# The first stage of an attention and mixture-of-experts kernel: a written order for VectorE, scores one unit ahead, weight conversions spread evenly

## The chip, the cores and the metric

The kernel runs on one core of a Trainium2 chip. The metric is the device time of one execution in microseconds (us); smaller is better. A unit of attention work below is half a batch (four heads); there are 16.

## The reference

```python
def sm_attn(qq, kk, vv):
    s = scale * np.matmul(qq, kk.transpose(0, 1, 3, 2))
    s = s - np.max(s, axis=-1, keepdims=True)
    a = np.exp(s)
    a = a / (np.sum(a, axis=-1, keepdims=True) + 1e-09)
    return np.matmul(a, vv)
p_packed = sm_attn(p, k, v)                 # 8 batches, 8 heads, 32 x 576 scores
out = sm_attn(q, p_packed, p_packed)
...
h = x @ w_in                                # 4608 x 512 x 2048
x = (h - np.tanh(h)) @ w_out
...
# top-2 of 8 experts, from x @ w_gate plus noise scaled with x @ w_noise:
h = np.maximum(x[mask] @ w1[e], 0.0)
out[mask] += top2_w[mask, k, None] * (h @ w2[e])
```

`w_in` and `w_out` come as 8-byte floats. The chip's engines work on 4-byte floats, so the kernel makes those from the two 4-byte words of each number by bit operations.

## The kernel before

There are three stages. The first (`phase_a`) computes `p_packed` for all 16 units and, beside it, converts 28 of the 32 chunks of `w_in` and `w_out` (128 x 512 numbers each, the "widenings"). The second (`phase_b`) does the other attention, the dense layer and the routing in steps; the third (`PhaseC`) is the experts. From some steps into the second stage on, TensorE (PE) works almost without a pause.

A unit of the first stage goes through these steps: `load_k` and `load_v` (SyncE, SP, issues the DMAs), `s1` (PE: 16 score matmuls into PSUM), `max1` (VectorE, DVE: a maximum over 576 columns and a scaling by -0.125), `exp1` (ScalarE, ACT), `recip1` (DVE, two instructions on 128 x 1), `t1` (PE: six transposes), `a1t` (ACT: copy of these to SBUF), `pv` (PE), `pz2` (DVE: scales `pv` into `Pz`), `pt` (PE transpose), `pt_out` (ACT copy into `PT`) and `pt_store` (a DMA). A chunk is `cv_load` (a DMA of 512 KB into `cvr`), part 0 (ACT, absolute value, line 69), part 1 (DVE, lines 73, 75, 76, 78 and 80), part 2 (ACT, line 84) and part 3 (DVE, lines 88 and 91).

`phase_a` runs a loop over `n`. In each turn of it the steps in the string `ORDER` are called in that order: the back half of unit n-1 (`t1` to `pts`), the front half of unit n, and the parts of two chunks, `p0` to `p3` for the first and `r0` to `r3` for the second; `pl` and `rl` load the two chunks of the next turn. `manual_schedule(engines=ENG)` keeps the written order on the engines in `ENG`. On every other engine a scheduler places the instructions, and before the change DVE is one of these. The 28 chunks go into the turns 0 to 13, two in each; the turns 14 and 15 have none.

Some buffers matter. The PSUM pool `psb` has two buffers under one tag for the scores `s1` and the transposes `tp`. `kT` and `v` have two buffers each, the raw chunks `cvr` have three.

`qs`, `qm`, `qx` and `qa` are the steps of the second attention's first block, in the turns 3 and 5 to 8: two PE score groups `sq`, DVE transposes into `st`, a maximum `mq` (DVE), a subtraction on GpSimd (POOL), an exponential (ACT), a sum (DVE), a multiplication (POOL) and a last transpose (DVE).

`consts_b` makes small constants for the routing. In the second stage's todo list its first part stands at step 1 and the rest, DMAs that fill two DRAM tensors, at step 3. In that stage `u_mm` (PE) fills both buffers of the PSUM pool `pm`, `u_hi` (ACT) and `u_lo` (DVE, tile `ul`) empty them, and `wo_step` widens the last four chunks (`cvc_b`, `cvf_b`).

Of the kernel before, what the change touches and what calls it, by code (L numbers as in the profile page):

```python
# [10 lines left out]
F32 = mybir.dt.float32  # L11
# [10 lines left out]
P = 128  # L22
# [78 lines left out]
    e.tensor_tensor(lo, src, hi.bitcast(F32), op=ALU.subtract)  # L101


ORDER = """t1 a1t s1 p0 lk p1 max1 p2 p4 pl r4 rec pv pz2 p3 exp1 pt r0 pto pts qs r1 lv qm qx r2 r3 qa rl""".split()
ENG = {mybir.EngineType.PE, mybir.EngineType.SP, mybir.EngineType.Activation}
NWA = 12


def phase_a(K, kT, v, w_in, w_out, wide_in, wide_out):
# [4 lines left out]
    with ExitStack() as ctx:  # L114
# [117 lines left out]
        def on(n, *fs):  # L232
            if 0 <= n < 16:
                for f in fs:
                    f(n)
# [5 lines left out]
              6: (lambda: Q.max(0), lambda: Q.sub(0), lambda: Q.exp(0)),  # L241
              7: (lambda: Q.sum(0), lambda: Q.mul(0)),
              8: (lambda: Q.out(0),)}
        load_k(0)
        cv_load(0)
        load_k(1)
        cv_load(1)
        load_v(0)
        for n in range(18):
            c0, c1 = 2 * n, 2 * n + 1  # L250
            ops = {
                "s1": lambda: on(n, s1), "max1": lambda: on(n, max1), "exp1": lambda: on(n, exp1),
                "t1": lambda: on(n - 1, t1), "a1t": lambda: on(n - 1, a1t), "rec": lambda: on(n - 1, recip1),
                "pv": lambda: on(n - 1, pv), "pz2": lambda: on(n - 1, pz2), "pt": lambda: on(n - 1, pt),
                "pto": lambda: on(n - 1, pt_out),
                "qs": lambda: n in (3, 5) and [f() for f in qs[n]], "qm": lambda: n == 6 and [f() for f in qs[n]],
                "qx": lambda: n == 7 and [f() for f in qs[n]], "qa": lambda: n == 8 and [f() for f in qs[n]],
                "pts": lambda: on(n - 1, pt_store),
                "lk": lambda: on(n + 2, load_k), "lv": lambda: on(n + 1, load_v),
                "p4": lambda: None, "r4": lambda: None,  # L260
                "p0": lambda: cv_step(c0, 0), "p1": lambda: cv_step(c0, 1), "p2": lambda: cv_step(c0, 2), "p3": lambda: cv_step(c0, 3),
                "r0": lambda: cv_step(c1, 0), "r1": lambda: cv_step(c1, 1), "r2": lambda: cv_step(c1, 2), "r3": lambda: cv_step(c1, 3),
                "pl": lambda: cv_load(c0 + 2) if c0 + 2 < 16 + NWA else None, "rl": lambda: cv_load(c1 + 2) if c1 + 2 < 16 + NWA else None,
            }
            for o in ORDER:
                ops[o]()
# [82 lines left out]
NSURE = 75  # L349


def consts_b(K, pp, pq, zero, w_gate, w_noise):
    nc, cp = K.nc, K.cpool
    K.tri = cp.tile([96, 96], BF, name="tri")
    nc.vector.memset(K.tri, 1.0)
# [17 lines left out]
    K.quarter = cp.tile([P, 1], F32, name="quarter")  # L373
    for q in range(4):
        nc.vector.memset(K.quarter[32 * q:32 * q + 32], float(q))
    pre = pq.tile([P, P, 2], F32, tag="st", name="pre")
    nc.vector.memset(pre, 0.0)
    nc.gpsimd.iota(pre[:, :, 0], pattern=[[1, P]], base=N, channel_multiplier=0, allow_small_or_imprecise_dtypes=True)
    yield
    tv = K.table.rearrange("(r l) two -> r (l two)", l=P)  # L380
    for r in range(0, TROWS, P):
        n = min(P, TROWS - r)
# [4 lines left out]
def pool(K, stack, name, bufs, **kw):  # L387
    return stack.enter_context(K.tc.tile_pool(name=name, bufs=bufs, reuse_waits="tile", **kw))


def phase_b(K, stack, wo_stack, qT, w1, w2, w_out, wide_out, noise, w_gate, w_noise, out):
# [7 lines left out]
    stage = stack.enter_context(ExitStack())  # L399
    K.WI = pool(K, stage, "b_wi", 1, side="right").tile([P, 4, FF], F32, name="WI")  # L400
    Q = K.Q = Queries(K, qT, qp, wq, None)
    yield
    RAW, CVB = {}, {}

# [12 lines left out]
    with ExitStack() as ctx:  # L417
# [4 lines left out]
        gp = pool(K, ctx, "b_g", 4)  # L422
        Q.pools = pool(K, ctx, "b_a", 2)
        wp = pool(K, ctx, "b_w", 1)
        cpre = pool(K, ctx, "b_pre", 1)
        wo2 = pool(K, ctx, "b_wo", 16 - NWA)

        woh = wp.tile([P, 16, DM], FR, name="woh")
        wol = []

        zero = wp.tile([P, P], F32, name="zero")
        nc.vector.memset(zero, 0.0)
        ET = mybir.EngineType
        ctx.enter_context(tc.manual_schedule(engines={ET.PE, ET.Activation, ET.DVE, ET.SP}))
        UT, GT, ACC, LG, PACE = {}, {}, {}, {}, [None]
# [243 lines left out]
        def at(t, f, *args):  # L679
            todo.setdefault(t, []).append((f, args))  # L680
# [36 lines left out]
            wol.append((wo2 if i < 16 - NWA else K.wo_pool).tile([P, DM], FR, tag="wo", name=f"wol{i}"))  # L717
            split(K, woh[:, i], wol[i], K.wof[i], "act", "pool" if i % 2 else "dve")

        consts = consts_b(K, cpre, wq, zero, w_gate, w_noise)  # L720
        at(1, next, consts)
        at(3, next, consts, None)

        def wo_step(i, p):
# [545 lines left out]
```

## Time and profile before

| | before |
|---|---|
| median of 3 runs | 1775.44 us (1774.39 to 1779.5) |
| the profiled execution, its own time | 1771.26 us |
| its span from the first to the last instruction | 1769.5 us |
| mean granted TensorE clock over the span | 0.956 of full |
| first stage, from the start to the last `Pz` | 0 to 146.34 us |
| first DVE instruction of the second stage on `ul` | 148.45 us |

The profiled execution is 4.18 us below the median of the runs. Times in the trace count from the start of the span. In a row of the timeline the first number is the start and the second the duration, both in us; a bracket at the end tells how long the engine sat idle before it and what ended that.

### The profile page before, as it was taken

How to read it: one execution, taken by the hardware profiler on the slowest of the kernel's cores; microseconds unless marked ns; L12 is line 12 of the kernel's file. 1: busy time of each engine (PE TensorE's matmuls, PEld its weight loads, DVE VectorE, ACT ScalarE, POOL GpSimd, SP SyncE). 2: the span in 40 equal slices, each digit the busy share in tenths (PEclk: the TensorE clock that was granted, in tenths of full speed). 3: DMA queues.
4: the chain of work that ended last, by engine and by line, in shares of the span. 5: the costliest groups of instructions: out<-in, count | busy, mean ns of one | idle time of the engine just before them, and what ended most of it. 6: DMA issues, size and time to landing. Idle time of an engine off the chain costs nothing. (4 is left out here: it accounts for less than half of the span.)

```text
span 1769.5 us, 29373 instructions
## 1 busy us (share of the span) xinstructions
PE 1633.7 (92%) x9942; PEld 1384.1 (78%) x9942; DVE 1198.9 (68%) x3090; ACT 871.1 (49%) x1850; POOL 569.2 (32%) x557
## 2 busy tenths in 40 slices
PE   5667999999999999999569699999999999999996
PEld 3345899898989898989557588888888888888885
DVE  7896978887878788866257366666666666666652
ACT  3454555555555555543134255555555555555552
POOL 0001200121212121223524644555454444444421
PEclk8668999999999999999779899999999999999998
DMA  8783467787867687722132656523672236722631
GB/s 275 237 271 109 131 218 228 218 241 213 242 223 229 213 239 219 238 95 83 23 112 43 233 176 196 152 48 56 230 238 49 49 67 220 239 50 49 206 62 26
DMA packets 145079, 285.22 MB, mean 161 GB/s; under 512 B 19618, under 2 KB 69066, under 8 KB 140316
## 3 DMA queue, kind: packets, MB, share of 16 engines
q1 hardware_dynamic: 121100, 243.78, 41.8%
q0 software_dynamic: 23824, 39.51, 12.3%
q8 instruction: 80, 1.31, 0.3%
q14 instruction: 75, 0.61, 0.1%
HBM read 687.34 MB, written 107.59 MB: 449 GB/s over the span
## 5 line engine op out<-in xcount | busy, mean ns | idle before, releaser
L1068 PE MATMUL ph<-w0s,xh 128*128 128x512 f32 x1200 | 378.5, 397 | 10.2 <-DVE h L1070 9.6
L1086 ACT ACTIVATE ht<-h 32x256 f32<-32x256 f32 x600 | 249.2, 415 | 267.4 <-issue 131.2
L1101 PE MATMUL py<-w1s,hh 128*128 128x512 f32 x1200 | 371.2, 390 | 2.3 <-ACT hh L97 2.3
L930 POOL DMA_INDIRECT x<-x1d,gidxm x276 | 265.4, 961 | 315.4 <-DVE xt L939 249.0
L500 PE MATMUL acc<-gh,woh 128*128 128x288 f32 x1024 | 302.9, 296 | 7.7 <-issue 7.6
L500 PE MATMUL acc<-gh,wol 128*128 128x288 f32 x1024 | 303.1, 296 | 7.0 <-issue 6.8
L500 PE MATMUL acc<-gl,woh 128*128 128x288 f32 x1024 | 301.9, 295 | 4.7 <-issue 4.7
L1070 DVE STREAM_TRANSPOSE h<-ph 128x512 f32<-128x512 f32 x150 | 107.4, 716 | 281.8 <-PE ph L1068 235.5
L1068 PEld LDWEIGHTS ph<-w0s,xh 128*128 128x128 f32 x1200 | 227.3, 190 | 64.3 <-DVE h L1070 11.2
L1101 PEld LDWEIGHTS py<-w1s,hh 128*128 128x128 f32 x1200 | 225.9, 188 | 50.9 <-ACT hh L97 3.2
L1068 PE MATMUL ph<-w0s,xl 128*128 128x512 f32 x600 | 236.8, 395 | 1.7 <-issue 1.7
L1101 PE MATMUL py<-w1s,hl 128*128 128x512 f32 x600 | 235.4, 392 | 2.1 <-DVE hl L101 1.3
L665 POOL DMA_INDIRECT table<-d,qi x96 | 91.8, 956 | 384.1 <-DVE g L484 151.6
L500 PEld LDWEIGHTS acc<-gl,woh 128*128 128x128 f32 x1024 | 193.5, 189 | 7.6 <-issue 7.6
L500 PEld LDWEIGHTS acc<-gh,woh 128*128 128x128 f32 x1024 | 193.7, 189 | 7.3 <-issue 7.3
L500 PEld LDWEIGHTS acc<-gh,wol 128*128 128x128 f32 x1024 | 193.3, 189 | 7.3 <-issue 7.3
L1084 DVE TENSOR_SCALAR ht<-h 32x256 f32<-32x256 f32 x600 | 185.7, 310 | 11.1
L97 ACT ACTIVATE gh<-g 128x288 fp32r<-128x288 f32 x256 | 113.5, 443 | 145.9 <-DVE g L484 143.9
L482 ACT ACTIVATE t<-h 128x288 f32<-128x288 f32 x256 | 104.1, 407 | 132.6 <-PE h L475 98.7
L475 PE MATMUL h<-a2h,uh 128*128 128x288 f32 x512 | 159.3, 311 | 9.8 <-DVE g L484 7.0
L484 DVE TENSOR_TENSOR g<-h,t 128x288 f32<-128x288 f32 x256 | 115.3, 450 | 61.2 <-ACT t L482 49.7
L475 PE MATMUL h<-a2l,uh 128*128 128x288 f32 x512 | 152.0, 297 | 1.1 <-issue 1.1
(235 smaller groups left out, 2495.6 us busy)
## 6 DMA issues: line engine op xcount, KB each, us to landing
w0s<-wsp SPq DMA_DIRECT2D x140, 2048.0 KB
w1s<-wsp SPq DMA_DIRECT2D x140, 2048.0 KB
wsp<-wt SPq DMA_DIRECT2D x128, 512.0 KB
wt<-in_w_dram SPq DMA_DIRECT2D x128, 256.0 KB
kT<-in_kT_dram SPq DMA_DIRECT2D x16, 608.0 KB
out_dram<-zero SPq DMA_DIRECT2D x37, 256.0 KB
v<-in_v_dram SPq DMA_DIRECT2D x16, 576.0 KB
q<-in_qT_dram SPq DMA_DIRECT2D x32, 288.0 KB
```

The costliest lines, as they stand in the source:

```text
L97: nc.scalar.activation(hi, src, AF.Copy)
L475: nc.tensor.matmul(h[:, :TN], u[:, G, fs], x[:, G, :], start=(n == 0), stop=(n == 5))
L482: nc.scalar.activation(t, h[:, :TN], AF.Tanh)
L484: PACE[0] = nc.vector.tensor_tensor(g, h[:, :TN], t, op=ALU.subtract).ins
L500: nc.tensor.matmul(ACC[ch][d][:, :TN], w[:, d * P:(d + 1) * P], x, start=(f == 0 and n == 0), stop=(f == 15 and n == 2))
L665: ins = nc.gpsimd.indirect_dma_start(out=K.table, out_offset=IO(ap=qi[:, i:i + 1], axis=0), in_=d[:, i, :], in_offset=None, oob_is_err=True)
L930: g = K.nc.gpsimd.indirect_dma_start(out=x[:, b, :], out_offset=None, in_=rows, in_offset=IO(ap=gidx[:, c, b:b + 1], axis=0))
L1068: K.nc.tensor.matmul(p, xx[:, d * P:(d + 1) * P], w[:, fc, ws, d, :], start=(n == 0), stop=(n == 11))
L1070: V.transpose(h[:, 2 * fc:2 * fc + 2].rearrange("p g n -> p (g n)"), p)
L1084: V.tensor_scalar(dst, src, 0.0, None, op0=ALU.max)
L1086: K.nc.scalar.activation(dst, src, AF.Relu)
L1101: K.nc.tensor.matmul(p, xx[:, f * P:(f + 1) * P], w[:, f // 4, ws, f % 4, :], start=(n == 0), stop=(n == 23))
```

## The change

It does four things in the first stage. DVE joins the engines that keep the written order, with a new `ORDER`. Turn n now issues `s1` of unit n+1, after `a1t` of unit n-1; `s1(0)` comes before the loop. `chunks(n)` gives each of 16 turns one or two chunks: one in the turns 0, 4, 8 and 12, two in the others. And the routing constants are made before the first stage, with only the `pre` tile (a memset and an iota) left at step 3.

```diff
-ORDER = """t1 a1t s1 p0 lk p1 max1 p2 p4 pl r4 rec pv pz2 p3 exp1 pt r0 pto pts qs r1 lv qm qx r2 r3 qa rl""".split()
-ENG = {mybir.EngineType.PE, mybir.EngineType.SP, mybir.EngineType.Activation}
+ORDER = """p0 lk pl t1 p1 a1t qm max1 s1 p2 pv r0 p3 exp1 rl lv r1 qx rec pz2 pt r2 pto pts qs r3 qa""".split()
+ENG = {mybir.EngineType.PE, mybir.EngineType.SP, mybir.EngineType.Activation, mybir.EngineType.DVE}
...
+        def chunks(n):
+            lo, hi = (min(16 + NWA, (16 + NWA) * k // 16) for k in (n, n + 1))
+            return tuple(lo + i if lo + i < hi else None for i in range(2))
+
         load_k(0)
         cv_load(0)
         load_k(1)
-        cv_load(1)
+        cv_load(chunks(0)[1])
         load_v(0)
-        for n in range(18):
-            c0, c1 = 2 * n, 2 * n + 1
+        s1(0)
+        for n in range(17):
+            c0, c1 = chunks(n)
+            d0, d1 = chunks(n + 1)
             ops = {
-                "s1": lambda: on(n, s1), "max1": lambda: on(n, max1), "exp1": lambda: on(n, exp1),
+                "s1": lambda: on(n + 1, s1), "max1": lambda: on(n, max1), "exp1": lambda: on(n, exp1),
...
-                "pl": lambda: cv_load(c0 + 2) if c0 + 2 < 16 + NWA else None, "rl": lambda: cv_load(c1 + 2) if c1 + 2 < 16 + NWA else None,
+                "pl": lambda: cv_load(d0), "rl": lambda: cv_load(d1),
...
     for q in range(4):
         nc.vector.memset(K.quarter[32 * q:32 * q + 32], float(q))
-    pre = pq.tile([P, P, 2], F32, tag="st", name="pre")
+    yield
+    pre = pp.tile([P, P, 2], F32, tag="st", name="pre")
     nc.vector.memset(pre, 0.0)
     nc.gpsimd.iota(pre[:, :, 0], pattern=[[1, P]], base=N, channel_multiplier=0, allow_small_or_imprecise_dtypes=True)
-    yield
...
     Q = K.Q = Queries(K, qT, qp, wq, None)
+    zero = wq.tile([P, P], F32, name="zero")
+    nc.vector.memset(zero, 0.0)
+    consts = consts_b(K, wq, zero, w_gate, w_noise)
+    next(consts)
     yield
...
-        consts = consts_b(K, cpre, wq, zero, w_gate, w_noise)
-        at(1, next, consts)
         at(3, next, consts, None)
```

DVE in a turn of the first stage before the change, from the `Pz` of unit 3 on; the chunk's parts stand among each other and among the unit's own steps:

```order
L216 SCALAR_TENSOR_TENSOR Pz_393<-pv_380,rs_318,mask 128x128
L75 TENSOR_SCALAR cva_365<-cvc_360 128x512
L192 TENSOR_SCALAR rs_398<-rs_398 128x1
L76 SCALAR_TENSOR_TENSOR cva_365<-cvr_296,cva_365 128x512
L193 RECIPROCAL rs_398<-rs_398 128x1
L80 TENSOR_SCALAR cvt_370<-cva_365 128x512
L88 TENSOR_TENSOR cvf_368<-cvf_368,cvt_370 128x512
L180 TENSOR_REDUCE nm_457<-s_4_436 128x1
L91 TENSOR_TENSOR WI<-cvf_368,cva_365 128x512
L73 TENSOR_SCALAR cvc_402<-cvc_402 128x512
L78 TENSOR_SCALAR cvf_416<-cvr_340 128x512
L75 TENSOR_SCALAR cva_413<-cvc_402 128x512
```

DVE after the change, the second half of turn 2 and the beginning of turn 3:

```order
L73 TENSOR_SCALAR cvc_331<-cvc_331 128x512
L75 TENSOR_SCALAR cva_343<-cvc_331 128x512
L76 SCALAR_TENSOR_TENSOR cva_343<-cvr_258,cva_343 128x512
L78 TENSOR_SCALAR cvf_346<-cvr_258 128x512
L80 TENSOR_SCALAR cvt_348<-cva_343 128x512
L194 TENSOR_SCALAR rs_256<-rs_256 128x1
L195 RECIPROCAL rs_256<-rs_256 128x1
L218 SCALAR_TENSOR_TENSOR Pz_352<-pv_318,rs_256,mask 128x128
L88 TENSOR_TENSOR cvf_346<-cvf_346,cvt_348 128x512
L91 TENSOR_TENSOR WI<-cvf_346,cva_343 128x512
L73 TENSOR_SCALAR cvc_362<-cvc_362 128x512
L75 TENSOR_SCALAR cva_376<-cvc_362 128x512
```

Now an instruction mostly reads what the one ahead of it wrote, and the next turn's first widening stands right behind this turn's last.

PE at the beginning of the first stage before the change:

```order
L175 MATMUL s_0_133<-kT_123 32x288 x8
L199 MATMUL tp_182<-ident,a_0_162 96x128 x6
L175 MATMUL s_1_191<-kT_127 32x288 x8
L211 MATMUL pv_220<-v_131,a1T_189 64x128 x12
L221 MATMUL pt_240<-ident,Pz_233 128x128
L199 MATMUL tp_262<-ident,a_1_237 96x128 x6
L175 MATMUL s_2_271<-kT_144 32x288 x8
```

And after it:

```order
L177 MATMUL s_0_157<-kT_149 32x288 x8
L177 MATMUL s_1_183<-kT_153 32x288 x8
L201 MATMUL tp_208<-ident,a_0_195 96x128 x6
L177 MATMUL s_2_228<-kT_168 32x288 x8
L213 MATMUL pv_238<-v_155,a1T_223 64x128 x12
L223 MATMUL pt_274<-ident,Pz_272 128x128
L201 MATMUL tp_288<-ident,a_1_255 96x128 x6
```

The scores of unit 2 now follow the transposes of unit 0, not those of unit 1. Since `s_1` is still held then, `s_2` takes the buffer of `tp` of unit 0 and waits until `a1t` on ACT has copied it.

DVE some steps into the second stage before the change, from the second `g` up to `ul` of the second `u`:

```order
L484 TENSOR_TENSOR g_1_1497<-h_1_1488,t_1_1495 128x288
L355 MEMSET tri 96x96
L358 MEMSET ones 96x128
L362 TENSOR_SCALAR ebase<-eio 128x8
L364 TENSOR_SCALAR eio_1508<-eio 128x8
...
L375 MEMSET quarter 32x1 x4
L377 MEMSET pre 128x256
L73 TENSOR_SCALAR cvc_b_1463<-cvc_b_1463 128x512
...
L450 TENSOR_TENSOR ul_1_1481<-u_1_0_1470,uh_1_1480 128x512
```

And after it:

```order
L492 TENSOR_TENSOR g_1_1518<-h_1_1509,t_1_1516 128x288
L73 TENSOR_SCALAR cvc_b_1484<-cvc_b_1484 128x512
L75 TENSOR_SCALAR cvc_b_1484<-cvc_b_1484 128x512
L76 SCALAR_TENSOR_TENSOR cvc_b_1484<-wor_1482,cvc_b_1484 128x512
L78 TENSOR_SCALAR cvf_b_1523<-wor_1482 128x512
L80 TENSOR_SCALAR cvf_b_1523<-cvc_b_1484 128x512
L458 TENSOR_TENSOR ul_1_1502<-u_1_0_1491,uh_1_1501 128x512
```

Twelve instructions on constants have left this place; the memset of `pre` now stands behind the fourth `g`.

## Rows read from the trace of the kernel before

**Rows 1.** Busy time of the engines in two stretches, TensorE clock, DMA share, GB/s

```profile
5.84:139.36 133.52, 84.58 (x686) 52.20 (x679) 115.89 (x278) 59.77 (x116) 2.68 (x2) 0.71 0.81 261
139.36:148.45 9.09, 7.72 (x92) 4.33 (x90) 2.10 (x9) 3.62 (x9) 0.00 (x0) 1.00 0.68 177
```

**Rows 2.** What DVE waited for from 5 to 148 us: in total, times, longest

```profile
DVE nm L180 <- PE s L175: 15.0, 11, 1.7
```

**Rows 3.** Timeline of DVE, first stage, instructions in a row

```profile
9.92 0.42 DVE L73 TENSOR_SCALAR cvc<-cvc 128x512 f32<-128x512 f32 x1
10.25 0.69 DVE L88 TENSOR_TENSOR cvf<-cvf,cvt 128x512 f32<-128x512 f32 x1
10.85 0.42 DVE L75 TENSOR_SCALAR cva<-cvc 128x512 int32<-128x512 int32 x1
...
15.51 0.42 DVE L73 TENSOR_SCALAR cvc<-cvc 128x512 f32<-128x512 f32 x1
15.97 0.43 DVE L75 TENSOR_SCALAR cva<-cvc 128x512 int32<-128x512 int32 x1
...
17.62 0.69 DVE L88 TENSOR_TENSOR cvf<-cvf,cvt 128x512 f32<-128x512 f32 x1
18.34 0.69 DVE L91 TENSOR_TENSOR WI<-cvf,cva 128x512 f32<-128x512 f32 x1
```

**Rows 4.** Timeline of DVE, the end of the first stage

```profile
140.93 0.76 DVE L180 TENSOR_REDUCE nm<-s 128x1 f32<-128x576 f32 x1 [1.40 <-PE s L175]
141.72 0.15 DVE L181 TENSOR_SCALAR nm<-nm 128x1 f32<-128x1 f32 x1
142.37 0.35 DVE L216 SCALAR_TENSOR_TENSOR Pz<-pv,rs,mask 128x128 f32<-128x128 f32 x1 [0.50 <-PE pv L211]
...
146.34 0.35 DVE L216 SCALAR_TENSOR_TENSOR Pz<-pv,rs,mask 128x128 f32<-128x128 f32 x1 [3.14 <-PE pv L211]
```

**Rows 5.** Timeline of all engines around the `Pz` of unit 1

```profile
26.09 0.35 DVE L216 SCALAR_TENSOR_TENSOR Pz<-pv,rs,mask 128x128 f32<-128x128 f32 x1 [0.60 <-PE pv L211]
26.36 0.42 DVE L75 TENSOR_SCALAR cva<-cvc 128x512 int32<-128x512 int32 x1
...
26.50 0.47 PE L221 MATMUL pt<-ident,Pz 128*128 128x128 f32 x1 [0.45 <-DVE Pz L216]
...
26.76 1.49 PE L199 MATMUL tp<-ident,a 128*96 128x128 f32 x6
...
27.01 0.28 ACT L226 ACTIVATE PT<-pt 128x128 f32<-128x128 f32 x1 [0.52 <-PE pt L221]
```

**Rows 6.** Timeline of ACT and SP: third chunk's first part, a constant's DMA issue

```profile
14.45 0.68 ACT L69 ACTIVATE cvc<-cvr 128x512 f32<-128x512 f32 x1 [3.31 <-DMA cvr<-in_w_in_dram]
...
144.83 0.50 SPq L369 DMA_DIRECT2D wgraw<-in_w_noise_dram  x1
```

**Rows 7.** Timeline of PE and ACT: scores, transposes' copy and `pv` of one unit

```profile
60.94 2.15 PE L175 MATMUL s<-kT 64*32 64x288 f32 x16
...
61.98 0.79 ACT L204 ACTIVATE a1T<-tp 96x768 f32<-96x768 f32 x1
...
63.02 2.19 PE L211 MATMUL pv<-v,a1T 96*64 96x128 f32 x24
```

**Rows 8.** Timeline of PE, POOL and DVE: the second attention's first block

```profile
58.35 1.21 PE L299 MATMUL sq<-q,pt 64*32 64x288 f32 x16
...
65.05 1.53 POOL L315 TENSOR_TENSOR st<-st,mq 128x576 f32<-128x576 f32 x1 [60.64 <-DVE mq L311]
...
65.48 1.38 DVE L78 TENSOR_SCALAR cvf<-cvr 128x512 int32<-128x512 int32 x1
```

**Rows 9.** Timeline of DVE and PE at the second stage's beginning

```profile
154.07 1.19 DVE L362 TENSOR_SCALAR ebase<-eio 128x8 f32<-128x8 f32 x1
...
158.34 1.28 DVE L450 TENSOR_TENSOR ul<-u,uh 128x512 fp32r<-128x512 f32 x2
...
159.08 1.06 PE L441 MATMUL u<-WI,pt 64*32 64x512 f32 x1 [6.10 <-DVE ul L450]
```

More of the change, by code (lines that the diff above doesn't have):

```diff
@@ L134, in cv_load @@
         def cv_load(i):
+            if i is None:
+                return
             if i < 16:
@@ L259, in phase_a @@
                 "lk": lambda: on(n + 2, load_k), "lv": lambda: on(n + 1, load_v),
-                "p4": lambda: None, "r4": lambda: None,
                 "p0": lambda: cv_step(c0, 0), "p1": lambda: cv_step(c0, 1), "p2": lambda: cv_step(c0, 2), "p3": lambda: cv_step(c0, 3),
                 "r0": lambda: cv_step(c1, 0), "r1": lambda: cv_step(c1, 1), "r2": lambda: cv_step(c1, 2), "r3": lambda: cv_step(c1, 3),
-                "pl": lambda: cv_load(c0 + 2) if c0 + 2 < 16 + NWA else None, "rl": lambda: cv_load(c1 + 2) if c1 + 2 < 16 + NWA else None,
+                "pl": lambda: cv_load(d0), "rl": lambda: cv_load(d1),
             }
@@ L349, with consts_b @@
 NSURE = 75
-def consts_b(K, pp, pq, zero, w_gate, w_noise):
+def consts_b(K, pp, zero, w_gate, w_noise):
     nc, cp = K.nc, K.cpool
@@ L424, in phase_b @@
         wp = pool(K, ctx, "b_w", 1)
-        cpre = pool(K, ctx, "b_pre", 1)
         wo2 = pool(K, ctx, "b_wo", 16 - NWA)
@@ L429, in phase_b @@
         wol = []
-        zero = wp.tile([P, P], F32, name="zero")
-        nc.vector.memset(zero, 0.0)
         ET = mybir.EngineType
```

## The prediction

> **What bounds the kernel now.** The list of the chain that ended last begins in the experts and says nothing of the first stage, so I read that stage by windows, then DVE's waits, then single instructions. In the first stage DVE is the fullest engine, 115.9 of 133.5 us, with the DMA engines 0.81 busy at 261 GB/s and PE at a mean granted clock of 0.71, a mix of 1.2 and 2.4 GHz [rows 1]. Most of what DVE loses there is 15.0 us in 11 waits of `max1` for the scores [rows 2]. After the last widening, from 139.36 us on, DVE has almost nothing left, and two units drain one behind the other. Then the second stage starts, with a hole on PE. After that PE has hardly a pause, so what the time up to there loses or gains should reach the end one to one. The question is when the last `Pz` comes, now 146.34 us, and how long the hole is.
>
> **What an instruction costs DVE.** Starts show that a step that doesn't read its predecessor's output costs less than one that does. Unrelated, a 512-wide integer or scalar step takes 0.33 us start to start (9.92 to 10.25) and a two-input step 0.60 (10.25 to 10.85). Reading the step ahead, line 75 starts 0.46 after line 73, and line 91 starts 0.72 after line 88 [rows 3]. The scheduler's order mixes chunks, and pays mostly the lower prices; the written order puts a chunk's steps in a row. Front of a chunk (73, 75, 76, 78, 80): 0.46 + 0.46 + 0.61 + 0.33 + 0.34 = 2.20, where the 0.61 is line 76 ahead of an unrelated step (0.60 by the row). Back (88, 91): 0.72 + 0.60 = 1.32. `max1`: 0.79, the scaling waiting for the whole reduction (140.93 to 141.72), and 0.12, its length of 0.15 less some overlap with an unrelated step [rows 4]. `recip1`: two such steps of 0.15, each with the 0.04 after its end that a dependent step waits (15.97 less 15.51 and 0.42), 0.38. `Pz`: 0.27 to the next start [rows 5]. A chunk is 3.52 and a unit 1.56, against 3.13 and about 1.19 at the unrelated prices. Over 28 chunks and 16 units the written order adds 10.9 + 5.9 = 16.8 us of DVE time. That takes back what the removed 15.0 us of score waits give.
>
> **A turn after the change.** I count from a `Pz` (time Z) to the next. DVE goes on with the back of the second chunk until Z + 0.27 + 1.32 = 1.59. The next front needs ACT's line 69, which in the written order stands behind `pt_out`, which needs `pt`, which needs this `Pz`: `pt` starts at Z + 0.41 and `PT` at Z + 0.92 with PE at 1.2 GHz [rows 5], about 0.1 earlier at 2.4 GHz; 0.18 later line 69 starts, takes 0.68 [rows 6], and DVE starts about Z + 1.76. Two-chunk turn: 1.76 + 2.20 + 0.91 + 1.32 + 2.20 + 0.38 = 8.77. One-chunk turn: 1.76 + 2.20 + 0.91 + 1.32 + 0.38 = 6.57 on DVE. But there PE may be later: `t1` runs from Z + 0.67 to 2.16 [rows 5], the copy `a1t` (0.79) must end before `s1` may have its buffer, then come `s1` (2.15) and `pv` (2.19) [rows 7], with overlaps about Z + 7.4 at 1.2 GHz. At 2.4 GHz DVE is later. I take 7.0 as the mean.
>
> **The start.** The first chunk comes as before, some 0.9 us later for the two constants' DMA issues (0.50 the second, the first a little shorter) ahead of it. The second chunk is no longer loaded in front; it stands behind the third `kT`, where the third chunk stood, whose line 69 started at 14.45 [rows 6]. One chunk of 524,288 bytes less is ahead of it: 261/0.81 = 322 GB/s at full share, so 1.6 us earlier, and 0.9 later. Line 69 starts about 13.75, DVE 14.45, and the first `Pz` comes 7.01 later, at 21.5. DVE idles some 2 us ahead of it.
>
> **The second attention's block** stands on DVE in the written order too. Turn 5: the transposes wait for `sq` (1.21) behind `pt`, +2.3. Turn 6: `mq`, then POOL's 1.53, ACT's exponential (some 0.7, as line 69 over nearly as many columns) and line 84 behind it before DVE's back of the first chunk, +2.8. Turn 7: reduction, two small steps, and POOL's second operation, which stretches a DVE step as line 78 here from about 0.45 to 1.38 [rows 8], +1.5. Turn 9: one split, +0.7. Sum 7.3; if ACT and POOL hide better, 2.5.
>
> **The sum.** The 15th `Pz` comes in turn 15: 21.5 + 11 x 8.77 + 3 x 7.0 + 7.3 = 146.3. One unit drains after it: 4.0 us at 2.4 GHz as in the rows (142.37 to 146.34) [rows 4], 5.4 at 1.2, taken as 4.7. So the last `Pz` is at 151.0, 4.7 later than now. The first `u` matmuls stand behind `pt` now, +0.2. In the hole, 6.1 us now, the constants leave the path to `ul`: `ebase` starts at 154.07, takes 1.19 because POOL works on a tile then, and `ul` comes at 158.34 and frees PE at 159.08 [rows 9]. The widening that moves up meets the same POOL work (as line 78 did), so I take 1.2 us saved and not the full 2.7 that the constants span. Small edits cost nothing: the constants' memsets at the start run before any chunk is there, cover 5 us; `pre`'s memset moves behind a `g`, and its DMAs are read only by scatters far later. Net: 4.7 + 0.2 - 1.2 = +3.7 us. From the profiled execution's 1771.26 that is 1775.0; this execution is 4.18 below the median of the runs, so 1779.1, rounded 1779. A measurement can tell about 0.3%, 5.3 us, from no change: I forecast no change, on the slow side. With the bounds of start, POOL, clock and drain, this case alone holds 1774 to 1785. Chance 0.62.
>
> **A rule against the prices.** The rows show 0.46 against 0.33 and 0.72 against 0.60 [rows 3]. The Trainium skill, page "VectorE: DVE Perf Modes", section "The DRAIN you can't avoid", says that the next step starts only when the pipe is empty, and that eight copies took the same with a semaphore after each as with one at the end, so that order would be free. By that rule the 0.39 per chunk and 0.37 per unit vanish, and the time would be that of rival one.
>
> **Rivals.** *One: neighbours cost nothing.* A turn is then 1.76 + 1.93 + 0.73 + 1.20 + 1.93 + 0.12 = 7.67, eleven of them save 12.1, the short ones 1.2 (PE holds them), the start 1.0: 3.7 - 14.3 = -10.6, 1765, faster. The rows speak against it. Chance 0.08. *Two: the waits hide.* The second block costs 2.5 and not 7.3, short turns 6.6, the drain 4.0 at 2.4 GHz: 3.7 - 4.8 - 1.2 - 0.7 = -3.0, 1772. For it speaks that PE was at full clock from 139 us on [rows 1]. Chance 0.16, a quarter of it faster. *Three: the loads bind.* SP issues in order, and the next `kT` and chunk stand behind `pt_store`, which waits for ACT at the turn's end. A two-chunk turn moves 622,592 + 2 x 524,288 + 589,824 + 65,536 = 2.33 MB, 7.2 us at 322 GB/s, under 8.77; it binds below 265 GB/s, and the stage's mean is 261 with gaps [rows 1]. At 240 a turn takes 9.7, and 14 turns add 13: 1792, slower. Chance 0.14, nearly all of it slower.
>
> **How the numbers follow.** Of the main case 0.18 lies beyond +5.3 us and 0.44 within. Slower: 0.18 + 0.12 = 0.30. Faster: 0.08 + 0.04 = 0.12. Same: 0.58. The range 1768 to 1788 leaves out half of rivals one and three and a little of the main case's ends.
>
> **What would show it.** `Pz` to `Pz` about 8.8 us in two-chunk turns and about 7 in the others; DVE waiting for ACT's line 69 some 0.2 us in most turns and 1.5 after a short one; no waits for scores; the first `Pz` near 21.5 and the last near 151; line 75 0.46 behind line 73. In the second stage the hole should be near 5 us. Wrong would make it: chunks that land late (DVE waits behind ACT's wait for DMA), or turns nearer 7.7.

## The result and the profile after

The changed kernel takes 1786.26 us (median of 18 runs, 1778.47 to 1791.69), the kernel before 1774.7 us on the same chips (18 runs, 1765.22 to 1779.5). The ratio is 1.0072, 95% interval 1.0058 to 1.0085: slower by 0.7%, about 12.8 us (the two medians lie 11.6 apart). The profiled execution has a span of 1784.8 us.

Chips differ by over 2% (the kernel before has a median of 1733 us on one and 1770 us on another), so kernels timed on different chips are compared by their ratio to the kernel before on the same chip. Times of the first stage agree better between chips: turns that an edit does not touch come out nearly the same (8.82 and 8.68 us for the second and third turn here and in e4 below, 8.81 and 8.67 in e12). I follow three marks through it: the `Pz` of units 0 to 15, the last of them, and the first `u` matmul behind the hole on PE, called u_2 below (159.08 us in [rows 9]). The stretch between the last two `Pz` is called the drain, the one from the last `Pz` to u_2 the handover.

The windows of the changed kernel (start:end, length, busy time and instructions of PE, PEld, DVE, ACT and POOL, granted clock, DMA share, GB/s), beside [rows 1]:

```profile
8.29:154.22 145.93, 92.31 (x726) 58.52 (x727) 123.22 (x282) 62.83 (x119) 2.31 (x2) 0.70 0.78 246
154.22:163.38 9.16, 7.44 (x44) 3.07 (x42) 0.58 (x4) 1.71 (x4) 0.00 (x0) 0.50 0.05 14
```

The first stage has become 12 us longer while the DMA engines moved less per us, and the stretch behind the last widening runs at a granted clock of 0.50, that is 1.2 GHz, where before it ran at 1.00.

What DVE waited for from 5 to 165 us (in total, times, longest), beside [rows 2]:

```profile
DVE cvc L73 <- ACT cvc L69: 14.4, 9, 5.2
DVE Pz L218 <- PE pv L213: 6.7, 4, 4.1
DVE ul L458 <- ACT uh L454: 4.5, 1, 4.5
DVE st L313 <- PE sq L306: 1.8, 1, 1.8
DVE cvf L88 <- ACT cvf L84: 1.7, 1, 1.7
```

The 15.0 us of waits for scores are gone. In their place stand waits for ACT's line 69. The first, 3.64 us, is the load of the first chunk; the longest, 5.2 us, is new.

The timeline of DVE in the first turn, beside [rows 3]:

```profile
8.29 0.43 DVE L73 TENSOR_SCALAR cvc<-cvc 128x512 f32<-128x512 f32 x1 [3.64 <-ACT cvc L69]
8.75 0.43 DVE L75 TENSOR_SCALAR cva<-cvc 128x512 int32<-128x512 int32 x1
9.21 0.69 DVE L76 SCALAR_TENSOR_TENSOR cva<-cvr,cva 128x512 int32<-128x512 int32 x1
9.82 0.42 DVE L78 TENSOR_SCALAR cvf<-cvr 128x512 int32<-128x512 int32 x1
10.16 0.42 DVE L80 TENSOR_SCALAR cvt<-cva 128x512 int32<-128x512 int32 x1
...
11.35 0.68 DVE L88 TENSOR_TENSOR cvf<-cvf,cvt 128x512 f32<-128x512 f32 x1
12.07 0.69 DVE L91 TENSOR_TENSOR WI<-cvf,cva 128x512 f32<-128x512 f32 x1
```

The written order pays 0.46, 0.46 and 0.72 us where a step reads its predecessor's output, as counted. Five two-chunk turns without other work take 8.68 to 8.84 us from `Pz` to `Pz`; the turns 13 and 14, also without, take 9.20 and 9.23.

The timeline of SP and ACT around chunk 8:

```profile
40.93 0.33 SPq L232 DMA_DIRECT2D ptd<-PT  x1
41.35 0.38 SPq L287 DMA_DIRECT2D pt<-ptd  x1
41.78 1.31 SPq L294 DMA_DIRECT2D q<-in_qT_dram  x2
43.13 0.60 SPq L162 DMA_DIRECT2D kT<-in_kT_dram  x1
43.83 0.84 SPq L146 DMA_DIRECT2D cvr<-in_w_in_dram  x2
...
51.93 0.66 ACT L69 ACTIVATE cvc<-cvr 128x512 f32<-128x512 f32 x1 [3.78 <-DMA cvr<-in_w_in_dram]
```

Line 69 of chunk 8 waits 3.78 us for its chunk. That was issued at 43.83, behind three loads for the second attention (`pt`, and `q` in two pieces) that `ORDER` puts at the end of the turn before.

The timeline of DVE and PE at the end of the stage, beside [rows 4] and [rows 9]:

```profile
152.54 0.35 DVE L218 SCALAR_TENSOR_TENSOR Pz<-pv,rs,mask 128x128 f32<-128x128 f32 x1
...
158.54 0.35 DVE L218 SCALAR_TENSOR_TENSOR Pz<-pv,rs,mask 128x128 f32<-128x128 f32 x1 [4.06 <-PE pv L213]
...
163.38 1.29 DVE L458 TENSOR_TENSOR ul<-u,uh 128x512 fp32r<-128x512 f32 x2 [4.50 <-ACT uh L454]
...
165.39 1.96 PE L449 MATMUL u<-WI,pt 64*32 64x512 f32 x16
...
173.81 2.55 PE L449 MATMUL u<-WI,pt 64*32 64x512 f32 x16 [3.89 <-DVE ul L458]
```

The last `Pz` comes at 158.54, 12.20 later than before, and u_2 at 173.81, 14.73 later. The wait ahead of u_2 fell from 6.10 to 3.89 us, but the way from the last `Pz` to it grew from 12.74 to 15.27. The rest of the program keeps the loss: 14.73 at u_2, 15.2 between the two profiled executions at the end, and 12.8 by the ratio.

### The profile page after: what moved, and what is told of

Read it like the earlier page. It is cut to its first block, busy times and chain, and to the rows that moved or that the text cites. A ratio compares the mean times of both kernels' runs of the same rounds, so it can differ in the third digit from the quotient of the medians.

```text
span 1784.8 us, 29376 instructions
## 1 busy us (share of the span) xinstructions
PE 1645.2 (92%) x9942; PEld 1389.9 (78%) x9942; DVE 1205.6 (68%) x3090; ACT 872.9 (49%) x1850; POOL 567.5 (32%) x557
## 4 chain that ended last, share of the span: by engine, by line
PE 77%; DVE 13%; issue 3%; DMA 2%; ACT 2%; another core or an unknown queue 1%; POOL 1%; SPq 0%; DVEq 0%; POOLq 0%; ACTq 0%
PE ph L1074 21%; PE py L1107 21%; PE acc L508 19%; PE h L483 10%; PE u L449 2%; DVE cva L76 1%; DVE xl L101 1%; DMA cvr<-in_w_in_dram 1%; PE sq L306 1%; DVE g L492 1%; DVE ht L1090 1%; DVE cva L75 1%; DVE cvf L88 1%; DVE gl L101 1%
## 5 line engine op out<-in xcount | busy, mean ns | idle before, releaser
L1074 PEld LDWEIGHTS ph<-w0s,xh 128*128 128x128 f32 x1200 | 226.7, 189 | 64.6 <-DVE h L1076 10.5
L1090 DVE TENSOR_SCALAR ht<-h 32x256 f32<-32x256 f32 x600 | 185.9, 310 | 11.1
```

What stands on the lines that cost most here:

```text
L1074: K.nc.tensor.matmul(p, xx[:, d * P:(d + 1) * P], w[:, fc, ws, d, :], start=(n == 0), stop=(n == 11))
L1090: V.tensor_scalar(dst, src, 0.0, None, op0=ALU.max)
```

## The experiments

Each was timed beside the kernel before: e2 to e5 together on one chip, e1 and e6 to e8 together, e9 to e11 together, e12 by itself. u_2 is read from the profiled execution.

| kernel | ratio to before, 95% | last Pz, us | u_2, us |
|---|---|---|---|
| changed kernel | 1.0072 (1.0058 to 1.0085) | 158.54 | 173.81 |
| e1 constants alone | 0.9999 (0.9988 to 1.0010) | 146.96 | 158.31 |
| e2 no spread | 1.0058 (1.0041 to 1.0075) | 154.06 | 166.28 |
| e3 scheduler's DVE order | 1.0005 (0.9993 to 1.0017) | 148.05 | 163.07 |
| e4 late q | 1.0056 (1.0039 to 1.0072) | 154.46 | 169.74 |
| e5 interleaved | 1.0119 (1.0099 to 1.0139) | 162.66 | 177.68 |
| e6 and line 69 early | 1.0054 (1.0041 to 1.0067) | 153.15 | 167.91 |
| e7 e3 and e4 | 0.9991 (0.9977 to 1.0006) | 142.20 | 157.49 |
| e8 e2, e3 and e4 | 0.9958 (0.9944 to 0.9973) | 145.09 | 157.31 |
| e9 e8, scores not ahead | 1.0000 (0.9991 to 1.0009) | 148.47 | 160.69 |
| e10 e2, e4 and e6 | 1.0002 (0.9989 to 1.0016) | 145.39 | 157.61 |
| e11 e8, store later | 0.9942 (0.9924 to 0.9960) | 137.44 | 149.67 |
| e12 PE filled | 1.0088 (1.0073 to 1.0104) | 161.73 | 176.90 |

My theory after the result: the loss has three parts, which are the dependent neighbours in DVE's written order, the chunk that is late behind the second attention's loads, and the widening that the spread puts into the last turns, which leaves PE at 1.2 GHz in the drain. The rivals: the order inside DVE costs nothing, the loads bind in general, or the constants at the beginning do harm.

**e2, the spread undone.**

```diff
-            lo, hi = (min(16 + NWA, (16 + NWA) * k // 16) for k in (n, n + 1))
+            lo, hi = (min(16 + NWA, 2 * k) for k in (n, n + 1))
```

> The changed kernel with the 28 chunks two to a turn again, in turns 0 to 13, none in 14 and 15. Theory (the spread puts widening into the last turns, so that the last units drain at the low PE clock, and four short turns cost more than they give back): 14 turns of 8.8 us and two of 4 to 5 in place of 12 of 8.8 and four of 7.6; last Pz 4 to 7 us earlier than the changed kernel's 158.54, a granted clock near 1.0 in the drain, the way from the last Pz to the first ul 2 to 3 us instead of 4.84; in all 5 to 9 us less than the changed kernel, 1.002 to 1.005 of the kernel before. Rival (the spread costs nothing, the loss is DVE's written order and the late chunk alone): 1.007 again, last Pz within 2 us of 158.5. Rival (loads bind, the spread helps them): later than 158.5.

The last turn and the way to u_2 in windows of this kernel:

```profile
150.13:154.06 3.93, 2.56 (x32) 2.14 (x33) 0.57 (x4) 1.08 (x2) 0.00 (x0) 1.00 0.10 26
154.06:166.28 12.22, 6.53 (x51) 3.04 (x50) 7.33 (x14) 6.71 (x15) 1.42 (x1) 0.97 0.02 6
```

and the same two stretches of the changed kernel:

```profile
152.54:158.54 6.00, 4.63 (x32) 3.83 (x33) 1.87 (x6) 1.08 (x2) 0.00 (x0) 0.50 0.05 14
158.54:173.81 15.27, 10.59 (x51) 4.58 (x51) 7.43 (x14) 6.90 (x15) 1.35 (x1) 0.61 0.02 5
```

PE executes the same 32 and 51 instructions. In the last turn they take 4.63 instead of 2.56 us at half the clock, and the 2.07 us between them is the whole difference of the turn (6.00 less 3.93). On the way to u_2 PE is busy 4.06 us longer, DVE and ACT only 0.1 and 0.2, and the stretch is 3.05 longer. So the spread costs 5.1 us there. The last `Pz` comes 4.5 earlier than in the changed kernel and u_2 7.5. The ratio falls by less than expected, 0.0014, some 2.5 us, with intervals that overlap; the profile's 7.5 is at their edge. In the whole time the spread's cost shows clear of noise only in e7 against e8 below, which differ by this edit alone: 0.9991 against 0.9958, some 6 us, with intervals that don't touch.

**e3, DVE's order left to the scheduler.**

```diff
-ENG = {mybir.EngineType.PE, mybir.EngineType.SP, mybir.EngineType.Activation, mybir.EngineType.DVE}
+ENG = {mybir.EngineType.PE, mybir.EngineType.SP, mybir.EngineType.Activation}
```

> The changed kernel with DVE's order left to the scheduler again, as in the kernel before; scores ahead, spread and early constants stay. Theory (dependent neighbours and the turn's border cost 0.8 us or more a turn): DVE busy in the stage falls from 123.2 to about 116 us, two-chunk turns to about 7.7 us, last Pz 8 to 12 us earlier than 158.54, ratio to the kernel before 0.999 to 1.002. Rival (a step costs DVE the same behind a step that it depends on): busy and turns within 0.2 us of the changed kernel, ratio 1.006 to 1.008. Rival (loads bind): DVE's busy time falls but the Pz stay where they are, and DVE's waits behind ACT's waits for DMA grow by as much.

What DVE waited for in this kernel:

```profile
DVE Pz L218 <- PE pv L213: 10.8, 7, 5.0
DVE cvf L78 <- DMA cvr<-in_w_in_dram: 7.8, 3, 3.6
DVE cvc L73 <- ACT cvc L69: 2.9, 6, 1.1
DVE nm L182 <- PE s L177: 2.5, 5, 0.7
DVE cvf L78 <- DMA cvr<-in_w_out_dram: 2.5, 1, 2.5
```

Windows from 5 us to the last `Pz`, the changed kernel and this one:

```profile
5.00:158.54 153.54, 97.82 (x768) 61.72 (x769) 123.45 (x284) 64.30 (x121) 2.31 (x2) 0.70 0.76 243
...
5.00:148.05 143.05, 91.11 (x768) 58.23 (x769) 116.04 (x286) 61.19 (x121) 2.74 (x2) 0.68 0.84 261
```

Five undisturbed turns take 7.3 to 7.7 us, the last `Pz` comes 10.5 us earlier, and nearly the whole loss is gone (1.0005). DVE's busy time (the third busy time of a row) falls by 7.4 us, from 123.45 to 116.04, and its idle time by 3.1. The waits for chunks hardly fell: 14.4 us at line 73 in the changed kernel; here 2.9 at line 73 and 10.3 at line 78, which the scheduler puts first and which waits for the DMA itself. This kernel differs from the changed one in the order alone, so the written order costs 10 to 12 us. How much of that is neighbours, and how much a fixed place in the row, e5 and e6 ask.

**e4, the loads of pt and q one turn later.**

```diff
-ORDER = """p0 lk pl t1 p1 a1t qm max1 s1 p2 pv r0 p3 exp1 rl lv r1 qx rec pz2 pt r2 pto pts qs r3 qa""".split()
+ORDER = """p0 lk pl t1 p1 a1t qm max1 s1 p2 pv r0 p3 exp1 rl lv ql r1 qx rec pz2 pt r2 pto pts qs r3 qa""".split()
-        qs = {3: (lambda: Q.load_p(0), lambda: Q.load_q(0)),
+        qs = {4: (lambda: Q.load_p(0), lambda: Q.load_q(0)),
...
-                "qs": lambda: n in (3, 5) and [f() for f in qs[n]], "qm": lambda: n == 6 and [f() for f in qs[n]],
+                "qs": lambda: n == 5 and [f() for f in qs[n]], "ql": lambda: n == 4 and [f() for f in qs[n]], "qm": lambda: n == 6 and [f() for f in qs[n]],
```

> The changed kernel with the loads of pt and q of the second attention's early block moved one turn on, behind the chunk and v loads of turn 4. Theory (chunk 8 comes late because these three loads stand ahead of kT6 and of it in SP's queue): DVE's wait of 5.2 us for line 69 in turn 5 and ACT's 3.78 for DMA go away, turns 5 and 6 together 3 to 4 us shorter than 26.2, all later Pz 3 to 4 us earlier, 1.005 of the kernel before. Rival (loads bind in general): the wait moves to a later chunk, the 15th Pz stays within 1 us of 152.5, ratio 1.007. If sq comes too late then, turn 5 loses what it wins.

The timeline of this kernel at the same place:

```profile
41.11 0.33 SPq L232 DMA_DIRECT2D ptd<-PT  x1
41.49 0.42 SPq L162 DMA_DIRECT2D kT<-in_kT_dram  x1
42.01 0.87 SPq L146 DMA_DIRECT2D cvr<-in_w_in_dram  x2
...
48.09 0.66 ACT L69 ACTIVATE cvc<-cvr 128x512 f32<-128x512 f32 x1
```

The chunk is issued at 42.01, 0.9 us behind the store instead of 2.9, and line 69 waits for nothing. From `Pz` of unit 3 to that of unit 4 takes 8.71 instead of 12.59 us. The next one takes 14.21 instead of 13.61 (line 69 waits 2.87 for a chunk there), so a little of it moves on; u_2 gains 4.07, as expected. The ratio falls by 0.0016, to 1.0056 where 1.005 was expected, with intervals that overlap: the gain is shown in the first stage, and for the whole time it isn't clear of noise.

**e5, max1 and the first chunk's back shuffled into the fronts.** `dve`, `dve2` and `max1` become generators that yield behind each step, and two are run in turns.

```diff
...
-                "s1": lambda: on(n + 1, s1), "max1": lambda: on(n, max1), "exp1": lambda: on(n, exp1),
+                "s1": lambda: on(n + 1, s1), "max1": lambda: None, "exp1": lambda: on(n, exp1),
...
-                "p0": lambda: cv_step(c0, 0), "p1": lambda: cv_step(c0, 1), "p2": lambda: cv_step(c0, 2), "p3": lambda: cv_step(c0, 3),
-                "r0": lambda: cv_step(c1, 0), "r1": lambda: cv_step(c1, 1), "r2": lambda: cv_step(c1, 2), "r3": lambda: cv_step(c1, 3),
+                "p0": lambda: cv_step(c0, 0), "p1": lambda: mix(front(c0), max1_(n)), "p2": lambda: cv_step(c0, 2), "p3": lambda: None,
+                "r0": lambda: cv_step(c1, 0), "r1": lambda: mix(front(c1), back(c0)), "r2": lambda: cv_step(c1, 2), "r3": lambda: cv_step(c1, 3),
```

> The changed kernel with DVE's written order shuffled inside a turn alone: max1's two steps between the first chunk's front steps, and the first chunk's back steps between the second chunk's front steps, so that hardly a step reads its predecessor's output. Theory (0.13 to 0.15 us for each dependent neighbour that goes, about 5 a two-chunk turn, 2 to 3 in a short one): two-chunk turns 8.1 us instead of 8.8, DVE busy 6 to 8 us less than 123.2, last Pz 7 to 9 us earlier than 158.54, ratio 1.002 to 1.004. Rival (order inside DVE is free): turns 8.7 to 8.8, ratio 1.006 to 1.008.

It went the other way: 1.0119, undisturbed two-chunk turns of 9.05 to 9.14 us. One turn in the timeline of DVE and ACT (front steps are lines 81 to 92 here, the back 100 and 104, `max1` 208 and 210):

```profile
113.57 0.43 DVE L81 TENSOR_SCALAR cvc<-cvc 128x512 f32<-128x512 f32 x1
113.91 0.75 DVE L208 TENSOR_REDUCE nm<-s 128x1 f32<-128x576 f32 x1
...
115.98 0.42 DVE L92 TENSOR_SCALAR cvt<-cva 128x512 int32<-128x512 int32 x1
116.09 0.63 ACT L96 ACTIVATE cvf<-cvf 128x512 f32<-128x512 f32 x1 [1.86 <-DVE cvf L89]
...
116.63 0.65 ACT L69 ACTIVATE cvc<-cvr 128x512 f32<-128x512 f32 x1
...
117.32 0.43 DVE L81 TENSOR_SCALAR cvc<-cvc 128x512 f32<-128x512 f32 x1 [0.92 <-ACT cvc L69]
117.66 0.69 DVE L100 TENSOR_TENSOR cvf<-cvf,cvt 128x512 f32<-128x512 f32 x1
```

The price of neighbours did fall: 0.34 from line 81 to the next step where the changed kernel has 0.46, and the second front and the first back together, up to `recip1`, take 3.15 us instead of 3.52. DVE's busy time up to the last `Pz` fell by 4.9 us, to 118.56, where 6 to 8 were expected. But ACT's line 69 for the second chunk stands behind its step on the first (line 96 here, 84 before), and that needs DVE's front. In the changed kernel `max1` and the first back cover this time; shuffled into the fronts they don't, and DVE waits 0.92 us in this turn; its waits for line 69 come to 27.0 us in 21, from 14.4. My expectation looked at DVE's row alone.

**e6, the same with line 69 of the second chunk first on ACT.** The diff shows what it has beyond e5.

```diff
-ORDER = """p0 lk pl t1 p1 a1t qm max1 s1 p2 pv r0 p3 exp1 rl lv r1 qx rec pz2 pt r2 pto pts qs r3 qa""".split()
+ORDER = """p0 lk pl t1 p1 a1t qm max1 s1 r0 p2 pv p3 exp1 rl lv r1 qx rec pz2 pt r2 pto pts qs r3 qa""".split()
```

> As the kernel with the interleaved DVE order, but ACT's line 69 of the second chunk stands ahead of its line 84 of the first, so that it need not wait for DVE. Theory (the interleaving did take 0.7 us of DVE time from a two-chunk turn, and lost 0.9 because DVE then waited for ACT's second line 69, which max1 and the back of the first chunk had covered): that wait goes, two-chunk turns fall from 9.14 to about 8.1 us, last Pz 10 to 13 us earlier than 162.66, below 152, ratio 1.000 to 1.004. Rival (the interleaved order itself is slow): turns stay at 9 us or more, ratio 1.009 or more. Rival (loads bind): line 69 waits for DMA instead, turns 8.5 and more, ratio above 1.005.

Undisturbed two-chunk turns took 8.10 to 8.31 us, as expected. One of the last turns took 9.70 (line 69 waits 1.36 for its chunk there), and those of the second attention stayed. So the last `Pz` is at 153.15, not below 152, and the ratio 1.0054, above the 1.004 that I had allowed and in the range of the rival on loads: line 69 waits 14.7 us for chunks, against 11.7 in the changed kernel, so that a little of this rival holds. Against e5 it gained 9.5 us in the last `Pz`, and 5.4 against the changed kernel, about what DVE's busy time fell by (5.1, to 118.34). The interleaved order is not slow by itself; what it covered was missing.

**e1, the early constants alone.** The kernel before, with the parts of the change that touch `consts_b` and `zero`.

```diff
     Q = K.Q = Queries(K, qT, qp, wq, None)
+    zero = wq.tile([P, P], F32, name="zero")
+    nc.vector.memset(zero, 0.0)
+    consts = consts_b(K, wq, zero, w_gate, w_noise)
+    next(consts)
     yield
...
-        consts = consts_b(K, cpre, wq, zero, w_gate, w_noise)
-        at(1, next, consts)
```

> The kernel before with the early constants alone. Theory (at full PE clock the way from the last Pz to u_2 was 12.74 us before, and 12.22 in the kernel without the spread, which has the constants early as well; the start is up to 0.9 us later for two more loads on SP): 0.5 to 1.5 us faster or nothing, ratio 0.999 to 1.000, last Pz within 1 us of 146.3, the hole ahead of u_2 below 6.10 us. Rival (the early constants delay the first loads by more, or POOL's work beside DVE hurts): last Pz 1.5 us or more later, ratio 1.001 or more.

The last `Pz` came 0.62 us later and u_2 0.77 earlier; the wait ahead of u_2 fell from 6.10 to 4.71. The ratio is 0.9999. This piece neither costs nor brings anything that can be measured.

**e7 and e8, the repairs together.** e7 has the edits of e3 and e4, e8 those of e2 as well.

> DVE's order left to the scheduler and the loads of pt and q moved one turn on, both together. Theory (two separate losses, 11.6 us and about 3): turn 4 falls from 11.64 to 8 or 9 us, last Pz 3 to 4 us earlier than 148.05, ratio 0.998 to 0.999. Rival (with a faster DVE the loads bind everywhere): the late chunk only moves to another turn, last Pz within 1 us of 148, ratio 1.000 or more.

> As the one with the scheduler's DVE order and late q loads, and the chunks two to a turn in turns 0 to 13 again: scores ahead and early constants are what is left of the change. Theory (without widening in the last turns PE works at full clock there, which gives back 2 us per drained unit and 3 us between the last Pz and u_2): last Pz 2 to 4 us earlier than with the spread, 12.2 us from there to u_2 instead of 15, ratio 0.994 to 0.997, the fastest of all. Rival (two chunks in every turn are more than the loads can bring): DVE waits behind DMA in the turns up to 13, last Pz not earlier, ratio as with the spread or above.

(What the expectation of e7 calls turn 4 is the stretch from unit 3's `Pz` to unit 4's.) It fell from 11.64 to 6.37 us, and the last `Pz` came 5.9 earlier. e7's ratio, 0.9991, holds no change in its interval. e8 is faster than the kernel before, 0.9958. Its profiled execution was the slowest of its eight (1771.58 against a median of 1764.11), e7's nearly the fastest of its twelve (1763.82 against 1770.11), so that their `Pz` can't be set against each other, and that e8's last `Pz` came later than e7's says little. The handover can be: 12.22 us in e8, 15.29 in e7, as forecast.

**e9, the scores back in their own turn.** The diff is against e8.

```diff
-ORDER = """p0 lk pl t1 p1 a1t qm max1 s1 p2 pv r0 p3 exp1 rl lv ql r1 qx rec pz2 pt r2 pto pts qs r3 qa""".split()
+ORDER = """p0 lk pl t1 p1 a1t s1 qm max1 p2 pv r0 p3 exp1 rl lv ql r1 qx rec pz2 pt r2 pto pts qs r3 qa""".split()
...
-        s1(0)
...
-                "s1": lambda: on(n + 1, s1), "max1": lambda: on(n, max1), "exp1": lambda: on(n, exp1),
+                "s1": lambda: on(n, s1), "max1": lambda: on(n, max1), "exp1": lambda: on(n, exp1),
```

> As the fastest one so far (scheduler's DVE order, late q loads, two chunks a turn, 0.9958), but the scores in their own turn again, as in the kernel before. Theory (the scores ahead are what made it faster): DVE waits 8 to 14 us for the scores again, last Pz 4 to 8 us later than 145.09, ratio 0.999 to 1.003. Rival (the scheduler's order or the loads take up that time anyway): last Pz within 2 us of 145, ratio 0.994 to 0.998.

DVE's waits for the scores, in this kernel and in e8:

```profile
DVE nm L182 <- PE s L177: 16.8, 9, 2.5
...
DVE nm L182 <- PE s L177: 1.9, 2, 1.2
```

The waits for scores are back, and so is the time: 1.0000 against 0.9958. The scores ahead are worth 0.4%, some 7 us, where nothing takes it back.

**e10, DVE in a written order after all.** The edits of e2, e4 and e6.

> DVE in a written order after all: the interleaved order with ACT's second line 69 early, with late q loads and two chunks a turn. Theory (three separate losses of the changed kernel taken away in the written order: neighbours, late chunk, spread): two-chunk turns near 8.1 us, last Pz 141 to 147, ratio 0.996 to 1.000. Rival (a fixed order waits wherever a load is late, which the scheduler's order does not avoid either): last Pz 148 or later, ratio 1.001 to 1.004.

Two-chunk turns of 8.09 to 8.30 us, last `Pz` 145.39, ratio 1.0002. A written order without the three faults is as fast as the kernel before, and 0.4% behind the scheduler's. (That e8's last `Pz`, 145.09, is no earlier says little: its profiled execution was 7.5 us slower than its median.)

**e11, pt_store one turn later.** The diff is against e8.

```diff
-ORDER = """p0 lk pl t1 p1 a1t qm max1 s1 p2 pv r0 p3 exp1 rl lv ql r1 qx rec pz2 pt r2 pto pts qs r3 qa""".split()
+ORDER = """p0 lk pl pts t1 p1 a1t qm max1 s1 p2 pv r0 p3 exp1 rl lv ql r1 qx rec pz2 pt r2 pto qs r3 qa""".split()
...
-        for n in range(17):
+        for n in range(18):
...
-                "pts": lambda: on(n - 1, pt_store),
+                "pts": lambda: on(n - 2, pt_store),
```

> The fastest one so far with pt_store one turn later, behind the loads of the next kT and first chunk, so that these need not wait on SP for PT. Theory (SP in order: kT and the first chunk wait for PT at the turn's end, and ACT then waits 17.0 us in 7 waits for chunks at line 69): that wait falls to 9 us or less, last Pz 4 to 8 us earlier than 145.09, ratio 0.990 to 0.994. Rival (the DMA engines' rate binds, they are 0.86 busy): the waits stay above 13 us, last Pz within 2 us of 145, ratio 0.994 to 0.998.

ACT's waits at line 69, in this kernel and in e8:

```profile
ACT cvc L69 <- DMA cvr<-in_w_in_dram: 9.2, 3, 5.9
ACT cvc L69 <- DMA cvr<-in_w_out_dram: 0.9, 1, 0.9
...
ACT cvc L69 <- DMA cvr<-in_w_in_dram: 13.1, 5, 5.7
ACT cvc L69 <- DMA cvr<-in_w_out_dram: 3.9, 2, 3.4
```

The waits fell from 17.0 to 10.1 us, not quite to the 9 that I had expected. Of the 9.2 us, 5.92 is the first chunk and 2.17 the second. Later chunks cost 2 us in all (in e8 the third wait and those behind it came to 9.1). The last `Pz` is at 137.44, u_2 at 149.67, and the DMA engines are 0.89 busy at 277 GB/s from 5 to 140 us, against 0.86 and 269 in e8, so that the rate was not what held e8's chunks. The ratio, 0.9942, is the best of all, but just above the 0.990 to 0.994 of the theory, and its interval (to 0.9960) overlaps e8's. The last `Pz` came 7.65 us earlier than in e8, whose profiled execution was itself 7.5 slower than its median. So the shorter waits are shown, and that the store's place brings anything in the whole time is not.

**e12, PE's gaps filled.** The changed kernel; behind `pv` of units 9 to 14 the same 12 matmuls again, into a tile that nobody reads.

```diff
+            if 9 <= n < 15:
+                more = ps.tile([P, 512], F32, tag="ps", name=f"more{n}")
+                for i in range(6):
+                    for j in range(2):
+                        PE.matmul(more[64 * j:64 * j + 64, :P], t["a1T"][:, i, 64 * j:64 * j + 64], t["v"][:, i, P * j:P * j + P], start=(i == 0), stop=(i == 5))
```

> The changed kernel with PE's gaps filled in six units: behind pv of units 9 to 14 the same 12 matmuls once more into a tile that nobody reads. Theory (the drain and the way to u_2 are long because PE runs at 1.2 GHz there, and not because of the widening beside it): the granted clock is 1.0 from the last units on, the last turn falls from 6.00 to about 4 us, the way from the last Pz to u_2 from 15.27 to about 12.3, u_2 3 to 5 us earlier than 173.81, ratio 1.004 to 1.006. Rival (the widening beside it makes it long): the clock rises, and the last turn stays near 6 us and the way near 15, ratio 1.007 or, by the added matmuls, above. If the clock does not rise, the two stay undecided, and the added matmuls cost up to 1 us a turn.

Windows of this kernel, two stretches ahead of the drain and the drain itself:

```profile
110.00:130.00 20.00, 13.56 (x169) 10.12 (x166) 15.19 (x37) 7.81 (x16) 0.00 (x0) 0.82 0.75 226
130.00:140.00 10.00, 6.16 (x76) 4.49 (x73) 8.70 (x20) 4.91 (x10) 0.00 (x0) 0.89 0.93 281
...
160.00:170.00 10.00, 9.21 (x55) 3.56 (x51) 2.09 (x4) 2.67 (x6) 0.00 (x0) 0.50 0.02 7
```

The clock rose to 0.82 and 0.89 where the fill was (the changed kernel has 0.61 and 0.67 there), and was down at 0.50 again in the drain, behind unit 15, which has none. The last turn stayed at 5.99 us. So this run does not decide what it was made for, and the ratio is 0.0016 higher, with intervals that overlap. The case for the clock rests on the windows of e2.

## Why the prediction was right and wrong

The time lay in the range (1786.26 of 1768 to 1788), which is in part luck: the main case alone was put at 1774 to 1785, the range reached higher for the sake of the rivals, and what the sum missed went one way. The likeliest outcome did not come: I called no change, +3.7 us on the slow side, and it is +12.8 by the ratio. The mechanism named first was right, several sizes of the sum were not.

- **The written order takes back what the score waits give: right, and more than that.** Neighbours cost 0.46 and 0.72, a two-chunk turn 8.68 to 8.84 against 8.77, and the score waits vanished. e3 and e9 measure both sides: the written order costs 0.67% (e3 against the changed kernel), the scores ahead bring 0.42% (e9 against e8). I had set the two nearly equal, 16.8 against 15.0 us; of the 16.8, e3 gets 10.5 back at the last `Pz`. Rival one, 1765, is out: 0.46 against 0.34 in e5 for the step behind the same line. A step that reads its predecessor's output started behind that one's end (0.46 us after one that took 0.42), a step that doesn't ahead of it (0.33) [rows 3]. The Trainium skill, page "VectorE: DVE Perf Modes", section "The DRAIN you can't avoid", has the semaphore after each of eight copies cost nothing extra, and adds that "A next op that is not held starts earlier"; the trace agrees with the addition, and disagrees with taking the eight copies for dependent steps. But neighbours are not all of the order's cost. e6 wins 5.4 us in the last `Pz` without most of them, e3 10.5 with a scheduler, which also moves steps around whatever is late.
- **"Turn 5: the transposes wait for `sq`", +2.3: a late chunk was missing.** The two turns up to the `Pz` of units 4 and 5 were put at 22.64 together and took 26.20. In e4, without the loads of `pt` and `q` ahead of chunk 8, they take 22.92. The second attention's block itself was priced well. Rival three saw SP's order, but hung it on `pt_store` and on the mean rate in all turns; the `q` loads in one turn were the price here.
- **"One-chunk turn ... I take 7.0 as the mean": wrong choice.** They took 7.39, 7.77 and 7.55, and `Pz` waited for `pv` there (the 6.7 us of such waits above are 4.06 in the drain and 0.82, 0.87 and 0.98 in the three short turns). The bound by PE that I had worked out, 7.4 at 1.2 GHz, was the nearer one in all three. Together +1.7 us.
- **"One unit drains after it ... taken as 4.7", "+0.2", and the hole, "1.2 us saved".** Taken together these let the way from the 15th `Pz` to u_2 go from 16.71 us (142.37 to 159.08) to 16.4; it became 21.27. This is the step that failed most, 4.8 of the 11.0 us that I missed at u_2: 1.3 in the drain (6.00) and 3.5 in the handover (15.27). I took the drain between the two clocks and the handover at 2.4 GHz as before. Before the change the last two turns had next to no widening, took 4.00 and 3.97 us and had PE at 1.00 [rows 1]; the spread fills the first of these, and PE is at 0.50 in the drain. All five kernels with two chunks to a turn in turns 0 to 13 and none behind (e2, e8 to e11) have 3.92 or 3.93 us for the drain and 12.22 or 12.23 to u_2; all seven with the spread (the changed one, e3 to e7, e12) 5.98 to 6.00 and 14.76 to 15.29. That the spread lowers the clock is shown by this; by what of PE's work it does so is not, since e12 left it open.
- **The hole, "1.2 us saved", was priced well for the constants.** With them alone it fell by 1.4 us (6.10 to 4.71 in e1; 4.72 in e2, where the spread is undone). In the changed kernel it fell by 2.2, but slower `u` matmuls ahead of it (1.96 instead of 1.09 us) took more than that. In the whole time early constants by themselves brought nothing (e1).

The sum at u_2: 0.7 for the start, 3.6 for the late chunk, 1.7 for short turns, 0.3 for the other turns, 4.8 for drain and handover, 11.1 in all, against a miss of 14.73 less 3.7.

What stays open: how the written order's 10 to 12 us divide. 7.4 of them are DVE's busy time (e3), of which interleaving gave back 5 (e5, e6); how the rest divides between fixed places behind late chunks and ACT's row is not shown. Open is also whether the three repairs overlap: e2, e3 and e4 gain 7.5, 10.7 and 4.1 us at u_2 one by one and 16.5 together (e8), but e8's profiled execution was slower than its median, and by the ratio they gain 0.0014, 0.0067 and 0.0016 one by one and 0.0114 together.

## What to carry to other kernels

Before an order is written out for one engine, read what each of its steps covers on the others: moving `max1` and the first chunk's back won 0.7 us on DVE's row and lost 0.9 to ACT's. Spreading work evenly over a stage also takes away its idle end, and here only the kernels that kept that idle end ran the last unit and the next stage's first matmuls at 2.4 GHz. Follow the small loads too: three of them ahead of a chunk in one in-order queue cost 3.9 us in one turn.

## What the runs showed of the hardware that I had not expected

- The same 32 PE instructions took 2.56 us at a granted clock of 1.00 and 4.63 at 0.50. The drain took 3.92 to 3.97 us or 5.98 to 6.00 in all fourteen kernels, and nothing between.
- Where extra matmuls stood in PE's gaps, the granted clock was higher (0.82 and 0.89 instead of 0.61 and 0.67); in the drain, which had none, it was 0.50 (e12).
- From 5 to 140 us the DMA engines moved 258 GB/s in the changed kernel and 277 in e7 and e11, so that 258 was not the most they could move.
